# Three units' transposes of r and k moved from TensorE to DMA, the order of all steps changed, and the last output matmul cut into two column runs

## The chip, the cores and the metric

The kernel runs on one core of one Trainium2 chip. The metric is the device time of one execution in microseconds. A run of a kernel gives one such time; the times below are of several runs. A profile of one execution gives the rest: busy times of the five engines (TensorE or PE with its weight loads PEld, VectorE or DVE, ScalarE or ACT, GpSimd or POOL, SyncE or SP), what each instruction waited for, and the DMAs.

## The reference

Two parts follow one another. The first is a linear attention with decay (RWKV-5): per batch b and head h a 48 x 48 state is carried through 768 time steps. The second is a feed-forward block with a squared ReLU on the 3072 x 384 result.

```python
batch, n_heads, seq, head_dim = (4, 8, 768, 48)
for t in range(S):
    cur = np.einsum('bhd,bhe->bhde', u[None] * kt, vt)
    y[:, :, t] = np.einsum('bhd,bhde->bhe', rt, state + cur)
    state = w[None, :, :, None] * state + np.einsum('bhd,bhe->bhde', kt, vt)
...
n_tokens, d_model, d_ff = (3072, 384, 2048)
h = np.maximum(x @ w_in, 0.0)
return (h * h @ w_out).astype(np.float32)
```

Here x is y with the heads side by side. All inputs and the output are float32; the kernel computes its matmuls in bf16.

## The kernel before

**Units.** The 768 steps are cut into six chunks of 128, and each of the 4 batches gives one unit per chunk: 24 units of 128 tokens x 384 features. Unit i is chunk i // 4 of batch i % 4. Chunk by chunk the recurrence becomes matmuls. For a unit the steps are:

- `ld` (L320): r, k and v are loaded by SP, 192 KB each, into one of seven buffers each.
- `rh`, `kh` (L339, L336): r and k are scaled by powers of the decay and cast to bf16, on VectorE or GpSimd, into one tile `rk` with the heads padded to 64.
- The transposes of `rk` into `rkT`: either `T` (L363), eight 128 x 128 transposes on TensorE into a PSUM bank, followed by `Tc` (L260), a ScalarE copy of 128 x 1024 to SBUF; or `XB` (L369), one DMA transpose issued by SP, SBUF to SBUF. Before, units 0 to 8 and 11 use T and Tc, the other 14 use XB.
- `A` (L376): eight matmuls k^T r per head, two PSUM banks; `Bm` (L384): masked copies on VectorE.
- `P0`, `P1`, `du`, `dv` (L342, L346, L349, L354): the term with u, elementwise, on VectorE and GpSimd. `vb` (L260, L262) casts v.
- `Y` (L392, L394): the unit's output from state and masked scores; `xs` (L411) adds dv. `U` (L403), `ts` (L421), `S` (L424) bring the state to the next chunk; `S0` (L418) does so for the first chunk.
- x has to be transposed too: `X` (L429) on TensorE with the copy `xTc` (L260), or `xX` (L436), a DMA transpose on SP.

**Feed-forward.** Units 0 and 1 are groups 0 and 1 by themselves, then two units make a group: 13 groups. `F1` (L445) computes 512 columns' worth of x @ w_in for a group into one of two banks, `re` (L453 on ScalarE, L455 on VectorE) takes the ReLU, `sq` (L460 on ScalarE; L464, L462 on VectorE) the square, and `F2` (L472) accumulates a quarter of h*h @ w_out, four matmuls of 384 columns, for one unit into one of two output banks `bO`. After the fourth quarter `os` (L260 or L262) copies the bank to one of four SBUF buffers and `out` (L489) stores it. For the last unit, 22, `os` and `out` are split in two halves of 192 columns.

**Weights.** `lW` (L324) loads seven of the eight pieces of w_in in float32 by SP, `cW` (L260, L262) casts them to bf16; `W` (L333) lets GpSimd's queue load the eighth and all of w_out, cast on the way.

**What sets the order.** Nothing is scheduled by the framework: `ORDER` is a list of all steps, written out, each with its engine and its buffer (`XB.9:S/1` is the DMA transpose of unit 9, issued by SP, into rkT buffer 1). A loop at the end of the kernel emits the steps in the order of the list, and every engine runs its own steps in that order; semaphores make a step wait for its inputs and for its buffer to be free. An engine that waits holds up everything behind it in its queue. SP's queue carries the loads, the transposes and the outs; its DMAs share eight completion semaphores in turn, so that the ninth waits for the first to land. `Z` (L481) steps are matmuls of the identity on itself, which give no result; they fill TensorE's time during the start.

Of the kernel before, what the change touches and what calls it, by code (L numbers as in the profile page):

```python
# [32 lines left out]
sq.2.5:D2/5 re.2.7:A/4 S0.3:D F1.0.1:P/0 F1.2.3:P/1 re.0.1:D/0 F2.1.0:P/0 S0.1:D re.2.3:A/3 F1.1.1:P/0 sq.1.2:D2/6
sq.0.1:D2/7 ld.k.7:S/6 F1.2.0:P/1 re.1.1:A/5 F2.0.1:P re.2.0:A/0 sq.1.1:D2/8 F1.2.2:P/0 sq.2.4:A0/9 sq.2.0:D1/10
F2.1.1:P kh.4:D/4 F1.2.6:P/1 ld.v.5:S/4 rh.4:D P0.4:D/4 F2.1.2:P ld.r.7:S/6 re.2.2:D/5 P1.4:G F2.0.2:P re.2.6:D/1
sq.2.2:A0/11 F2.1.3:P ld.v.4:S/5 kh.5:G/5 sq.2.1:A0/12 sq.2.6:D1/13 F2.0.3:P os.1:A/0 du.4:D/4 ld.k.6:S/0 T.4:P/0
sq.2.3:A0/14 rh.5:D F2.2.0:P/0 os.0:A/1 P0.5:D/0 Tc.4:A/4 ld.r.6:S/0 T.5:P/3 P1.5:D F2.2.1:P kh.7:D/6 Tc.5:A/5
ld.v.7:S/6 A.4:P/1/2 du.5:D/0 F2.3.0:P/1 Bm.4.0:D/3 ld.k.9:S/2 A.5:P/0/3 vb.4:A/4 dv.4:G Bm.4.1:D/2 F2.3.1:P vb.5:A/5
ld.r.9:S/2 Bm.5.1:D/4 dv.5:G sq.2.7:A0/15 Y.4:P/1 Bm.5.0:D/5 F2.3.2:P rh.7:G ld.k.8:S/1 xs.4:D/4 U.4:P/2 Y.5:P/3
F2.2.2:P P0.6:G/1 ld.v.6:S/0 xs.5:D/0 X.4:P/0 ts.4:D/0 X.5:P/1 T.7:P/3 xTc.4:A/1 kh.6:D/1 ld.k.15:S/3 F2.2.3:P xTc.5:A  # L40
rh.6:D vb.7:A/6 U.5:P/2 P1.6:D F1.3.0:P/0 Tc.7:A/6 ld.k.10:S/4 ts.5:D/1 F1.3.1:P/1 kh.9:D/2 re.3.0:A/0 ld.v.9:S/2
T.6:P/0 P0.7:D/2 os.2:A/2 A.7:P/1/2 S.5:D re.3.1:A/5 ld.r.8:S/1 F2.3.3:P du.6:D/2 P1.7:G Tc.6:A/0 Bm.7.1:D/0 F1.3.3:P/0
sq.3.0:A0/16 rh.9:G ld.r.10:S/3 os.3:D/3 F1.3.4:P/1 re.3.3:A/2 Bm.7.0:D/1 A.6:P/3/0 P0.9:G/3 du.7:D/1 re.3.4:A/1
XB.9:S/1 F1.3.5:P/0 Bm.6.1:D/3 sq.3.1:A0/17 dv.7:G F1.3.6:P/1 Bm.6.0:D/2 re.3.5:A/3 F2.5.0:P/0 dv.6:G vb.6:A/7
ld.k.12:S/5 sq.3.3:A0/18 Y.7:P/2 out.3:S kh.10:D/3 re.3.6:A/4 Y.6:P/1 ld.v.8:S/3 S.4:G xs.7:D/1 F1.3.2:P/0 sq.3.5:A0/19
xs.6:D/2 F1.3.7:P/1 ld.v.11:S/1 kh.8:D/0 re.3.2:A/0 kh.15:D/4 U.6:P/0 X.6:P/3 sq.3.2:A0/20 X.7:P/2 rh.8:D F2.4.0:P/1
ld.r.12:S/4 re.3.7:A/5 rh.10:D F2.5.1:P xTc.6:A/2 sq.3.4:D2/21 P1.9:D xTc.7:A U.7:P/1 T.8:P/3 vb.9:A/2 out.0:S P0.8:D/4
F1.4.0:P/0 ts.6:D/1 ld.k.11:S/0 Tc.8:A/2 P1.8:G ts.7:D/0 F1.4.4:P/1 ld.r.13:S/5 du.9:D/3 re.4.0:A/2 F2.5.2:P kh.12:G/5
re.4.4:A/3 F1.4.6:P/0 ld.r.11:S/0 sq.3.6:A0/23 sq.3.7:D2/22 vb.8:G/3 du.8:D/4 A.9:P/2/0 sq.4.4:A0/24 A.8:P/1/3 S.6:G
re.4.6:A/0 F2.5.3:P ld.v.10:S/5 Bm.8.1:D/4 F1.4.3:P/1 dv.8:G Bm.8.0:D/5 os.5:A/3 ld.k.13:S/6 F1.4.5:P/0 Bm.9.1:D/1  # L50
re.4.3:A/1 dv.9:G Y.8:P/3 Bm.9.0:D/0 re.4.5:A/5 XB.10:S/3 F2.4.1:P P0.12:G/0 xs.8:D/3 sq.4.0:A0/25 Y.9:P/1 vb.11:A/1
kh.11:G/1 F1.4.1:P/1 xs.9:D/4 ld.v.13:S/4 X.8:P/0 F1.4.2:P/0 re.4.1:D/4 xTc.8:A/0 ld.r.15:S/6 F2.4.2:P rh.11:D
sq.4.1:A0/26 P1.12:D X.9:P/2 vb.10:A/0 F1.4.7:P/1 P0.10:D/1 ld.k.20:S/2 xTc.9:A sq.4.5:D2/27 F2.7.0:P/0 P0.11:D/2
re.4.7:A/3 ld.v.12:S/6 U.8:P/3 P1.10:D sq.4.3:A0/28 F2.4.3:P kh.13:D/6 re.4.2:A/2 F1.5.2:P/1 du.10:D/0 out.1:S os.4:A/1
rh.13:G sq.4.2:A0/29 ts.8:D/1 A.10:P/1/0 ld.k.17:S/1 F2.6.0:P/1 re.5.2:A/4 P1.11:G ld.k.14:S/5 F1.5.7:P/0 rh.12:G
F1.5.1:P/1 du.11:D/1 ld.k.16:S/4 re.5.7:A/5 T.11:P/2 rh.15:D re.5.1:A/1 F1.5.0:P/0 dv.10:G Bm.10.1:D/3 Tc.11:A/4
# [12 lines left out]
ts.12:D/1 ld.k.21:S/3 sq.6.6:A0/13 F2.9.3:P P1.18:G xs.13:D/3 sq.6.5:A0/15 ld.v.16:S/1 F2.10.0:P/1 Bm.14.1:D/2 dv.14:G
X.13:P/0 du.15:D/0 F2.10.1:P ld.r.20:S/4 P0.16:G/4 re.6.7:D/2 xTc.13:A Y.14:P/1 vb.15:A/6 F1.7.5:P/0 kh.20:G/6 xs.14:D/4  # L70
ld.k.22:S/6 os.9:A/0 F1.7.6:P/1 S.12:D A.16:P/2/3 xX.14:S/0 re.7.6:A/1 P1.17:G A.17:P/0/1 F2.11.0:P/0 sq.6.7:A0/16
Bm.17.1:D/1 sq.6.4:A0/17 S.13:G F1.7.1:P/1 ld.v.20:S/6 Bm.16.1:D/0 re.7.5:A/4 F2.11.1:P ld.k.19:S/5 Bm.17.0:D/2 dv.15:G
Y.15:P/1 re.7.1:D/3 ld.r.19:S/6 F1.7.0:P/0 xs.15:D/0 rh.20:G F1.7.3:P/1 re.7.0:A/0 ld.r.23:S/5 P1.16:D U.15:P/3
sq.7.1:A0/20 F2.10.2:P du.16:D/1 re.7.3:A/2 U.14:P/0 xX.15:S F1.7.2:P/0 P0.20:D/1 vb.16:A/3 dv.16:G Bm.16.0:D/3
sq.7.3:A0/18 F1.7.4:P/1 out.5:S re.7.2:A/5 rh.18:D F2.11.2:P vb.18:A/1 out.8:S sq.7.6:D2/21 re.7.4:A/3 F2.10.3:P
sq.7.5:D2/19 ld.r.21:S/2 kh.19:D/5 vb.17:A/2 F1.7.7:P/0 ld.k.23:S/1 sq.7.4:A0/22 rh.19:D Y.16:P/1 kh.22:D/4 re.7.7:A/2
Y.17:P/2 XB.19:S/4 xs.16:D/2 sq.7.2:A0/23 F2.11.3:P kh.21:D/2 os.10:A/3 F1.8.2:P/1 du.17:D/2 sq.7.0:A0/26 XB.18:S/6
ts.14:D/1 F1.8.0:P/0 dv.17:G re.8.2:A/1 F2.12.0:P/1 os.11:A/2 re.8.0:D/4 vb.20:G/0 sq.8.2:A0/25 F1.8.3:P/1 xX.16:S/1
# [31 lines left out]
    ld=["{0}{1}"],  # L110
# [7 lines left out]
def kernel(  # L118
# [66 lines left out]
    def bank(var, kind="b"):  # L185
        return banks[first[kind] + slot[var]]
# [85 lines left out]
    class Do:  # L272
# [206 lines left out]
        def Z(e, n, b):  # L479
            for _ in range(n):  # L480
                e.matmul(banks[b][:, 0:128], identity, identity, start=True, stop=True, skip_group_check=True)  # L481
# [60 lines left out]
```

## Time and profile before

| | |
|---|---|
| device time, median of 3 runs | 176.17 us (174.75, 176.17, 177.58) |
| span of the profiled execution | 174.6 us |
| what lies around its span | not listed; the fastest run is 0.15 us above it, the median 1.57 |
| TensorE busy | 164.3 us (94%), 1813 matmuls |
| of these F1 / F2 / T / A | 74.4 / 73.6 / 6.2 / 8.5 us busy |
| VectorE, ScalarE, GpSimd busy | 140.6, 109.4, 69.4 us |
| XB: issue to landing | 3.3 to 5.0 us, median 4.2, 14 times |
| SP's DMA queue | 26.20 MB, its packets 72.6% of 16 engines' span |
| first F1 / last matmul ends | 21.6 us / 171.07 us |

Busy time of an engine is the union of its instructions, which overlap by some tens of nanoseconds, so that counts times mean durations give more than the busy time. The chain that ended last is followed back from the last instruction through what released each step; it tells whose time the span is made of. The profile's times are from the start of the span.

### The profile page before, as it was taken

To read this page: it belongs to the slowest core of one execution; us is meant where nothing else is said; L and a number is where in the kernel's file an instruction comes from. 1 tells how busy PE (TensorE), PEld (TensorE's weight loads), DVE (VectorE), ACT (ScalarE), POOL (GpSimd) and SP (SyncE) were. 2 spreads that over 40 slices of the span, in tenths; PEclk is the share of its full clock that TensorE was granted. 3 is DMA by queue.
4 is the path that set the end of the run, shared out by engine and by line. 5 is a ranking of instruction groups with operands and counts; after the bars stand their busy time and mean duration, and the time that the engine had idled before them with its cause. 6 is when DMAs were issued, how large, how long until landed. Compare 5 with 4: busy or idle time off the path is not lost.

```text
span 174.6 us, 4605 instructions
## 1 busy us (share of the span) xinstructions
PE 164.3 (94%) x1813; PEld 127.1 (73%) x1813; DVE 140.6 (80%) x279; ACT 109.4 (63%) x203; POOL 69.4 (40%) x85
## 2 busy tenths in 40 slices
PE   3978599999999999999999999999999999999991
PEld 3967488866778777877767787777778677787760
DVE  5779677799899989999989898899988667853620
ACT  3578479549499987786677669669478142164410
POOL 5253834044366594925373960700950302000000
PEclk9999999999999999999999999999999999999999
DMA  4989999989799999999998989989931422110041
GB/s 99 228 194 240 320 200 237 207 155 213 144 205 177 231 217 165 233 157 252 152 214 187 195 164 220 160 196 230 164 94 26 158 90 71 24 45 4 0 165 61
DMA packets 102421, 28.36 MB, mean 162 GB/s; under 512 B 94840, under 2 KB 102400, under 8 KB 102400
## 3 DMA queue, kind: packets, MB, share of 16 engines
q1 hardware_dynamic: 100504, 26.20, 72.6%
q0 software_dynamic: 1744, 1.77, 6.3%
q8 instruction: 14, 0.23, 0.5%
q10 hardware_dynamic: 152, 0.10, 0.2%
q14 instruction: 7, 0.06, 0.1%
HBM read 20.46 MB, written 4.72 MB: 144 GB/s over the span
## 4 chain that ended last, share of the span: by engine, by line
PE 84%; DMA 6%; SPq 4%; POOL 1%; issue 1%; ACT 0%; DVE 0%; POOLq 0%
PE bank L472 36%; PE bank L445 36%; DMA wsa<-in_moe_w_in_dram 6%; SPq L320 4%; PE bank L376 3%; PE bank L394 2%; PE bank L392 2%; PE bank L403 2%; PE bank L363 2%; PE bank L429 1%; POOL W L262 1%; SPq L324 0%; POOL urow L218 0%; ACT vb L260 0%; DVE os L262 0%
## 5 line engine op out<-in xcount | busy, mean ns | idle before, releaser
L445 PE MATMUL bank<-xT,W 128*128 128x256 bf16 (+1 forms) x624 | 74.4, 264 | 2.3 <-ACT W L260 2.1
L472 PE MATMUL bank<-W,hq 128*128 128x384 bf16 x384 | 73.6, 326 | 0.0
L453 ACT ACTIVATE hr<-bank 128x512 bf16<-128x512 f32 x71 | 42.0, 597 | 36.8 <-PE bank L445 34.2
L445 PEld LDWEIGHTS <-W 128*128 128x128 bf16 x624 | 55.4, 98 | 12.6 <-ACT W L260 2.2
L472 PEld LDWEIGHTS <-hq 128*128 128x128 bf16 x384 | 35.6, 98 | 17.8
L460 ACT ACTIVATE hq<-hr 128x512 bf16<-128x512 bf16 x57 | 34.7, 629 | 2.5 <-DVE hr L455 2.2
L384 DVE TENSOR_TENSOR Bm<-bank,maskJT 128x512 bf16<-128x512 f32 x48 | 31.4, 682 | 3.1 <-PE bank L376 3.0
L346 POOL TENSOR_TENSOR P<-P,ub 128x384 f32<-128x384 f32 x14 | 15.2, 1087 | 30.2 <-DVE P L342 27.4
L354 POOL TENSOR_TENSOR dv<-ldv,du 128x384 f32<-128x384 f32 x19 | 16.4, 874 | 25.0 <-DVE du L349 21.0
L455 DVE TENSOR_SCALAR hr<-bank 128x512 bf16<-128x512 f32 x25 | 17.1, 688 | 11.2 <-PE bank L445 7.5
L464 DVE TENSOR_TENSOR hq<-hr 128x512 bf16<-128x512 bf16 x35 | 15.0, 456 | 1.7 <-ACT hr L453 1.7
L411 DVE TENSOR_TENSOR xs<-bank,dv 128x384 bf16<-128x384 f32 x24 | 13.2, 553 | 3.2 <-PE bank L394 2.5
L481 PE MATMUL bank<-identity 128*128 128x128 bf16 x139 | 11.1, 244 | 2.7 <-POOL identity masks.py:199 2.7
L260 ACT COPY os<-bank 128x384 f32<-128x384 f32 (+1 forms) x18 | 8.4, 469 | 8.1 <-PE bank L472 8.1
L342 POOL TENSOR_TENSOR P<-ldr,ldk 128x384 f32<-128x384 f32 x11 | 11.3, 1025 | 4.8 <-DMA ldr<-in_r_dram 4.8
L349 DVE TENSOR_REDUCE du<-P 128x8 f32<-128x384 f32 x24 | 12.9, 542 | 0.0
L260 ACT COPY rkT<-bank 128x1024 bf16<-128x1024 bf16 x10 | 10.1, 1016 | 3.4 <-PE bank L363 3.3
L481 PEld LDWEIGHTS <-identity 128*128 128x128 bf16 x139 | 9.8, 112 | 2.9 <-POOL identity masks.py:199 2.7
L424 POOL TENSOR_TENSOR S0W<-ts,WLm 128x384 bf16<-128x384 f32 x7 | 7.4, 1061 | 10.0 <-PE bank L472 6.7
L394 PE MATMUL bank<-vb,Bm 128*128 128x48 bf16 x192 | 10.8, 183 | 0.5 <-ACT vb L260 0.5
L394 PEld LDWEIGHTS <-Bm 128*128 128x128 bf16 x192 | 9.5, 96 | 1.5 <-issue 0.8
L260 ACT COPY xT<-bank 128x384 bf16<-128x384 bf16 x14 | 6.5, 478 | 5.1 <-PE bank L429 5.1
(62 smaller groups left out, 167.1 us busy)
## 6 DMA issues: line engine op xcount, KB each, us to landing
ldr<-in_r_dram SPq DMA_DIRECT2D x24, 192.0 KB, 3.8
ldk<-in_k_dram SPq DMA_DIRECT2D x24, 192.0 KB, 3.9
ldv<-in_v_dram SPq DMA_DIRECT2D x24, 192.0 KB, 3.6
out_dram<-os SPq DMA_DIRECT2D x23, 192.0 KB, 2.1
wsa<-in_moe_w_in_dram SPq DMA_DIRECT2D x7, 384.0 KB, 5.9
W<-in_moe_w_out_dram POOLq DMA_DIRECT2D x4, 384.0 KB, 7.6
rkT<-rk SPq DMA_TRANSPOSE x14, 4.2
W<-in_moe_w_in_dram POOLq DMA_DIRECT2D x1, 192.0 KB, 8.8
```

What stands on the lines that cost most here:

```text
L260: e.copy(o, a)
L346: e.tensor_mul(t, t, ub)
L354: e.tensor_mul(dvb[slot[f"dv{i}"]], loaded("v", i), t)
L384: e.tensor_mul(Bmb[slot[f"Bm{i}{h}"]], heads(bank(f"bA{i}{h}"), 128), mask_b)
L394: e.matmul(y[:, hc, D * h : D * (h + 1)], m[h][:, hc, :], vb[:, 2 * hc + h, :], start=(c == 0), stop=True, skip_group_check=True,)
L445: e.matmul(hp[:, fi, :], W1[f // 2][:, c, 128 * (f % 2) : 128 * (f % 2 + 1)], xt[:, c, :], start=(c == 0), stop=(c == CCH - 1), skip_group ...
L453: e.activation(hr, hp, AF.Relu)
L455: e.tensor_scalar_max(hr, hp, 0.0)
L460: e.activation(hq, hr, AF.Square)
L464: e.tensor_mul(hq, hr, hr)
L472: e.matmul(bank(f"bO{i}", "bO")[:, 0:d_model], hqb[slot[f"hq{g},{f // m}"]][:, at : at + L], W2[q][:, f % 4, :], start=(f == 0), stop=(f = ...
L481: e.matmul(banks[b][:, 0:128], identity, identity, start=True, stop=True, skip_group_check=True)
```

## The change

Three things, all in one file.

1. Units 7, 8 and 11 lose `T` and `Tc` and get `XB`: 24 matmul transposes and 3 ScalarE copies out, 3 DMA transposes on SP in (17 in place of 14).
2. `ORDER` is a new list. Nearly every step has another place, and many another engine: `kh` 13 times on VectorE and 11 on GpSimd (19 and 5 before), `rh` 15 and 9 (18 and 6), `P0` 16 and 8 (13 and 11), `dv` 4 and 20 (5 and 19), `re` 21 times on VectorE and 75 on ScalarE (25 and 71), squares 28 on VectorE and 68 on ScalarE (39 and 57), `os` 11 on VectorE and 14 on ScalarE (7 and 18), `cW` 4 on ScalarE and 3 on GpSimd (6 and 1), `vb` 17 on ScalarE, 5 on GpSimd, 2 on VectorE (19, 3, 2). Ten of the outs go to GpSimd's queue (none before). The number of Z matmuls stays 139. During the start, `ld.v.1` comes earlier on SP's queue, `wc` (two small loads of the decay) earlier, `ld.v.3` later, behind `lW.0.7` and `lW.0.4`.
3. Unit 22's four F2 steps become two `F2c` steps: columns 256 to 383 over all 16 pieces of h, in one output bank, then columns 0 to 255 in the other. The halves of `os` and `out` follow these columns (256 and 128 wide; 192 each before).

The pools, buffers and all other functions stay as they are. The diff, with ORDER cut to its places named here:

```diff
-T.7:P/3 ... Tc.7:A/6 ... T.8:P/3 ... Tc.8:A/2 ... T.11:P/2 ... Tc.11:A/4
+XB.7:S/6 ... XB.8:S/1 ... XB.11:S/4
...
-lW.0.6:S/0 ld.v.1:S/0 ld.k.3:S/3 ld.v.3:S/1 lW.0.1:S/1 ld.r.3:S/3 ld.v.0:S/2 ld.v.2:S/3 lW.0.0:S/2 lW.0.5:S/3 lW.0.7:S/0 lW.0.4:S/1 wc:S
+wc:S lW.0.6:S/0 lW.0.0:S/2 ld.v.0:S/2 lW.0.1:S/1 lW.0.5:S/3 ld.v.2:S/3 lW.0.7:S/0 lW.0.4:S/1 ld.v.3:S/1 lW.0.3:S/2
...
-F2.22.0:P/0 ... F2.22.1:P ... F2.22.2:P F2.22.3:P os.22.0:A/2 os.22.1:D out.22.0:A out.22.1:S
+os.23:A/1 out.18:S out.23:S F2c.22.1:P/1 os.22.1:D/3 F2c.22.0:P/0 os.22.0:A out.22.1:S out.22.0:A
...
-    F1=["bH{0},{1}"], os=["os{0}"], Wk=["WkP"], Wt=["WtP"],
+    F1=["bH{0},{1}"], F2c=["bO{0}{1}"], os=["os{0}"], Wk=["WkP"], Wt=["WtP"],
...
+        def F2c(e, i, h):
+            g, j = group_of[i]
+            n = len(GROUP[g])
+            m = 4 // n
+            c = part(h)
+            for f in range(FCH):
+                at = L * n * (f % m) + L * j
+                e.matmul(
+                    bank(f"bO{i}{h}", "bO")[:, c],
+                    hqb[slot[f"hq{g},{f // m}"]][:, at : at + L],
+                    W2[f // 4][:, f % 4, c],
+                    start=(f == 0), stop=(f == FCH - 1), skip_group_check=True,
+                )
...
         def os(e, i, half=None):
             c = part(half)
-            copy(e, osb[slot[f"os{i}"]][:, c], bank(f"bO{i}", "bO")[:, c])
+            o = f"bO{i}" if half is None else f"bO{i}{half}"
+            copy(e, osb[slot[f"os{i}"]][:, c], bank(o, "bO")[:, c])
...
     def part(half):
-        return slice(0, d_model) if half is None else slice(d_model // 2 * half, d_model // 2 * (half + 1))
+        return slice(0, d_model) if half is None else (slice(0, 256), slice(256, d_model))[half]
```

The first six ORDER lines show steps of the two lists, with all steps between them left out.

## The prediction

> **What bounds the kernel now.** I read the page first (busy shares, then the chain that ended last), then the chain's shares by line, TensorE's waits, busy time by stretch, and last the timeline of the start and of the end.
>
> ```profile
> span 174.6 us, 4605 instructions
> PE 164.3 (94%) x1813; PEld 127.1 (73%) x1813; DVE 140.6 (80%) x279; ACT 109.4 (63%) x203; POOL 69.4 (40%) x85
> ```
> ```profile
> by line: PE bank L472 36.2%; PE bank L445 35.7%; DMA wsa<-in_moe_w_in_dram 6.3%; SPq L320 4.0%; PE bank L376 3.4%; PE bank L394 2.2%; PE bank L392 2.0%; PE bank L403 1.9%; PE bank L363 1.5%; PE bank L429 1.2%; issue 1.0%; POOL W L262 0.5%;
> ```
> ```profile
> PE bank L481 <- POOL identity masks.py:199: 2.7, 1, 2.7
> PE bank L445 <- ACT W L260: 2.1, 1, 2.1
> PE bank L363 <- DVE Bm L384: 0.6, 1, 0.6
> PE bank L394 <- ACT vb L260: 0.5, 2, 0.3
> PE bank L376 <- ACT rkT L260: 0.4, 2, 0.2
> PE bank L445 <- POOL W L262: 0.3, 1, 0.3
> ```
> ```profile
> 45.00:65.00 20.00, 20.00 (x249) 15.90 (x245) 18.99 (x36) 17.70 (x34) 12.19 (x15) 1.00 1.03 197
> 65.00:85.00 20.00, 20.00 (x226) 15.47 (x223) 19.15 (x36) 15.91 (x33) 10.28 (x11) 1.00 1.14 204
> 145.00:165.00 20.00, 20.00 (x167) 15.21 (x165) 12.76 (x27) 7.00 (x13) 0.02 (x1) 1.00 0.11 32
> ```
>
> The columns of the last fence are stretch, its length, then TensorE, its weight loads, VectorE, ScalarE and GpSimd busy, the granted clock, DMA share and GB/s. The chain is 84% TensorE, 146.7 us of 174.6. All its waits stand before 25 us, where weights arrive; from there it is busy in every stretch at clock 1.00. A busy PE is not PE at its peak, so I also added up the pieces: (624-96) x 109 ns plus 96 x 55 ns of F1, 384 x 163 ns of F2 and the small matmuls give 147 us from the first F1 at 21.6 to the last matmul at 171.07, which is 149.4 us. Some 2 us are gaps. So **TensorE's own work bounds the kernel from 25 us on; VectorE is nearly full beside it (19 of 20 us); the start is bound by arriving weights.**
>
> **The change, part by part.** All sums are on the profiled 174.6 us, which is 0.15 below the fastest run shown and 1.57 below their median of 176.17. I carry differences over to the median.
>
> *T removed (3 units).* The chain's share of L363 is 1.5%, 2.62 us for the six units transposed there after 25 us: 0.437 us per unit, or 8 x 54.6 ns. Three units: **-1.31 us** on the bound engine. Three Tc (L260, mean 1016 ns) leave ScalarE, -3.05 us, beside other work: nothing.
>
> *XB added (3), on SP.* The row of the 14 there are:
>
> ```profile
> L369 SPq DMA_TRANSPOSE rkT<-rk x14: 1237/1542/2622, 51.6 to 123.6; - x14
> DMA to landing us min/median/max: 3.3/4.2/5.0
> ```
>
> SP is busy issuing for 1.5 us each; queued behind are loads and later transposes. SP loses ten outs (about 0.55 us each) and gains three XB (+4.6 us), so its sum falls. What matters is whether a transpose lands before A (L376) reads it. I give each step a **place**: the TensorE time of all steps listed before it in ORDER (F1 0.66, F2 0.65, T 0.44, A 0.30, Y 0.335, U 0.17, X 0.18, Z 0.056 each, all from the chain's rows). In the kernel before, places foretell issue times: XB of units 9, 10, 15 and 17 have places 41.1, 53.1, 68.8, 81.4, and the trace has them at
>
> ```profile
> 51.59 1.64 SPq L369 DMA_TRANSPOSE rkT<-rk  x1
> 63.46 2.62 SPq L369 DMA_TRANSPOSE rkT<-rk  x1
> 79.09 1.70 SPq L369 DMA_TRANSPOSE rkT<-rk  x1
> 92.41 1.25 SPq L369 DMA_TRANSPOSE rkT<-rk  x1
> ```
>
> always 10.3 to 11.0 us later. From XB's place to A's place the kernel before has 5.4 to 14.7 us, all over the landing's 5.0. The new order has 4.7, 3.3, 2.3, 2.3, 4.1 for units 7 to 11, 3.6 for 13, 2.9 for 14, 1.6 for 17, 3.6 for 19 and 3.9 for 21. Taken literally the shortfalls against 4.2 us are 1.9 (8 and 9 together, whose A are neighbours), 1.9, 0.1, 0.6, 1.3, 2.6, 0.6, 0.3: **9.3 us** of waiting. But the new list is not sorted by time (P0.17 stands at 94.9 though its inputs are there at about 90; out.16 at 155 though os.16 is at 130), and following inputs and SP's queue, most can go earlier: XB.17 waits behind xX.12, which needs xs.12 (place about 81.2), so it goes at 83 and lands at 87, where A.17 stands at 87.1; XB.9 goes at about 44.5 and lands at 48.7 against 50.3; XB.11 needs kh.11 at 57.1 and lands at 61.3 against 61.9. Left are several arrivals within half a microsecond of their use. Bounds 0 and +9.3; nearest to the first by this tracing: **+0.5**.
>
> The Trainium skill (VectorE: DVE Perf Modes, sections "The three transpose paths" and "Rules for kernel authors") speaks against the change: a 128x128 transpose belongs on TensorE if PSUM may be its destination, at 390 ns against 1309 ns by DMA. By its figures one XB of eight blocks would be an estimated 10.5 us, and the three added ones would come 5.8, 7.2 and 6.4 us late by their places, +19.4 us in the sum. The trace disagrees with that size: all eight land in 4.2 us.
>
> *Engine loads.* By counts and row means VectorE loses 9.5 us (kh -6 x 633 ns, rh -3 x 575, squares -11 x 430, their busy time over their count; re -4 x 688, dv -1 x 558; P0 +3 x 606, os +4 x 553). ScalarE gains 1.6 (Tc and copies off; squares +11 x 609, re +4 x 597). GpSimd gains about 17.5 (kh, rh, casts; ten outs). Over the whole span each stays under TensorE. By stage, though, VectorE's steps with places 30 to 50 sum to 23.5 us, against 22.5 before, and its busy total is 0.92 of such a sum since neighbours overlap: 21.7 us in 20. It must lag some 1.7 there, against 0.7 before, and steps off by the same amount in 60 to 80. Bounds 0 and +1.7 less what the lists already lead: **+0.2**.
>
> *Ten outs on GpSimd.* Nearest rows: its weight DMAs take 771 ns to issue and 7.6 us to land (384 KB, DMA share over 1); the same out from SP lands in 2.1 us. Behind an out wait kh, rh, dv of its queue, at 0.8 us each; and an os slot comes free only when its out has landed. os.11 (place 97.8) reuses the slot of out.8 (issued at about 91), os.12 (108.3) that of out.4 (about 104). At 2.1 us both are free in time; at 7.6 os.12 comes 3.7 us late. I take 2.1, the same transfer: **0**; the other end is a rival.
>
> *The start.* Of it the timeline shows
>
> ```profile
> 21.63 1.51 PE L445 MATMUL bank<-xT,W 128*128 128x128 bf16 x24 [2.06 <-ACT W L260]
> 24.15 0.51 PE L445 MATMUL bank<-xT,W 128*128 128x128 bf16 x6 [0.27 <-POOL W L262]
> ```
>
> Loads landed at 4.7 us (0.39 MB), 9.2 (1.18), 15.0 (2.56), 17.4 (3.15) and 23.2 (4.33), read off what waited for them. With the new order on that curve W_in pieces 0 and 1 are there at 15.0 and 17.4, F1.1.0 follows X.0 at about 20.0 (-1.6), and piece 7 is cast at 23.1 (-1.0). But ld.v.3 now stands behind lW.0.7 and lW.0.4 (4.72 MB, some 25 us), and Y.3 needs it on TensorE's queue: at 25.7, where its place of 15.0 would like 24.3. The shift (time less place) is then 10.7 us against 10.5 before: the gain is given back. GpSimd's own weight DMAs go 1.2 to 2 us later than before, behind vb.2 and cW.0.3, and with their 7.6 us to land are there 1 us or less before use. Bounds -1.2 (v3 by 24) and +1.5 (by 26.5, or W.1.3 late): **0**.
>
> *The end.* Before:
>
> ```profile
> 171.09 0.32 ACT L260 COPY os<-bank 128x192 f32<-128x192 f32 x1 [4.72 <-PE bank L472]
> 171.44 0.35 ACTq L489 DMA_DIRECT2D out_dram<-os  x1
> 171.44 0.36 DVE L262 COPY os<-bank 128x192 f32<-128x192 f32 x1 [2.39 <-ACT os L260]
> ```
>
> VectorE's half waits for ScalarE's (one PSUM bank), and its out goes last, 0.76 us after the last matmul. F2c puts the halves in two banks: 16 matmuls of 128 columns (56 ns each, as the F1 of one unit: 0.90 us), then 16 of 256 (1.72); together +0.02 to F2's 2.60. Columns 256 to 383 are copied under the second run; then one copy of 256 columns (between 319 ns for 192 and 477 for 384: 0.37) and its out: 0.42 us after the last matmul. **-0.3**.
>
> Sum: -1.31 + 0.5 + 0.2 + 0 + 0 + 0.02 - 0.3 = **-0.9 us**: 173.7 on the profile, **175.3** on the median.
>
> **Rivals.** (1) *Transposes land after their A*: TensorE, in order, waits at L376 with all of F1 and F2 behind it. It decides wherever the way from XB's issue to A is under 4.2 us. For it: the leads above, a DMA share already at 1.0 to 1.14, 3.3 to 5.0 us spread. Against: no transpose was late before. Half the literal shortfall, 4.7 in place of 0.5, gives 179.5; all of it 184. (2) *GpSimd's outs land late* (7.6 us): os.12 holds VectorE for 3.7 us, behind it rh.21, XB.21 and A.21: about 178.5. Against: half the size and no cast. (3) *The start's gain is kept* and 0.5 of the old gaps close: -1.31 - 0.3 - 1.2 - 0.5 = -3.3, 172.9. For it: F1 does start earlier. (4) *The change doesn't do what it says*: TensorE's freed 1.31 us become gaps, because VectorE (9.25 to 9.67 of every 10 us from 45 to 95) sets the pace: 175.9 with the end's gain. Against: it loses 9.5 us.
>
> **How the numbers follow.** Forecast 0.50 (173.9 to 177.0), late transposes 0.17, late outs 0.08, start kept 0.14, gain absorbed 0.11. The range runs from the kept start, 172.7, to just above half the late transposes, 180.0; left out are the literal 9.3 us and a start better than its bound. A measurement of this kernel can tell about 2%, 172.65 to 179.69. Faster needs more than rival 3's middle: 0.10. Slower: most of rival 1 and a part of 2: 0.18. Same: 0.72.
>
> **What would show it.** Right: L363 has 56 matmuls; TensorE's waits at L376 on a DMA under 1 us; first F1 near 20 us, a wait for ldv or vb near 25; no ScalarE wait before VectorE's last copy. Wrong: waits at L376 of over 1 us behind rkT's DMA, or at os behind out_dram, or gaps at Bm and xs. The sum is most easily upset by DMA arrivals, which I placed by one curve of one run.

## The result, and the profile after

The changed kernel takes 185.09 us (median of 4 runs, 184.64 to 185.99) against 175.95 for the kernel before beside it (4 runs, 174.75 to 177.58): a ratio of 1.056, 95% interval 1.051 to 1.060. It is slower by 9 us, and the forecast (175.3, range 172.7 to 180.0) missed on the far side. All ratios, and the medians and ranges of the experiments below, leave out disturbed runs (over 1.5% above the fastest of their kernel), and a ratio can differ a little from the quotient of two medians.

The page of the changed kernel, span, busy shares, TensorE's clock in 40 slices and DMA issues with their time to landing:

```profile
span 182.9 us, 4597 instructions
PEclk9999999999999998799999999999999999999999
out_dram<-os SPq DMA_DIRECT2D x13, 192.0 KB, 2.9
out_dram<-os POOLq DMA_DIRECT2D x10, 192.0 KB, 3.4
rkT<-rk SPq DMA_TRANSPOSE x17, 3.7
```

The chain's shares by line, and TensorE's waits (us in total, times, longest):

```profile
by line: PE bank L445 28.1%; PE bank L472 23.1%; DMA out_dram<-os 6.1%; ACT hr L453 4.9%; DMA ldv<-in_v_dram 3.7%; SPq L320 3.5%; DVE Bm L384 3.4%; issue 3.1%; PE bank L376 2.3%; DMA ldk<-in_k_dram 2.0%; PE bank L394 1.7%; PE bank L403 1.6%
```
```profile
PE bank L445 <- ACT hr L453: 1.9, 5, 0.6
PE bank L472 <- ACT os L260: 1.9, 1, 1.9
PE bank L403 <- DVE xs L411: 1.3, 1, 1.3
PE bank L394 <- POOL vb L262: 0.9, 1, 0.9
PE bank L376 <- ACT rkT L260: 0.8, 1, 0.8
PE bank L445 <- DVE hr L455: 0.7, 1, 0.7
PE bank L403 <- DVE Bm L384: 0.6, 1, 0.6
```

And the same three stretches as before (length, TensorE, weight loads, VectorE, ScalarE, GpSimd busy, clock, DMA share, GB/s):

```profile
45.00:65.00 20.00, 19.77 (x234) 15.42 (x231) 19.19 (x36) 14.69 (x29) 11.32 (x12) 1.00 1.01 199
65.00:85.00 20.00, 17.57 (x183) 12.81 (x182) 13.16 (x26) 14.34 (x29) 10.19 (x11) 0.91 0.85 163
145.00:165.00 20.00, 20.00 (x173) 14.82 (x171) 11.76 (x23) 9.44 (x17) 3.95 (x6) 1.00 0.18 55
```

The chain was 84% TensorE; now F1, F2 and the small matmuls make 62% of it, and an out's landing, the ReLU and loads stand in it. No wait of TensorE ends at a DMA transpose. The waits at L445, L472 and L403 are on banks and buffers: F1 for the ReLU that empties its bank, F2 for `os`, U for the reader of its bank. VectorE has 13 us of work in the 20 between 65 and 85: it is kept waiting, not full.

To see where the time went I took the shift (start less place) of every TensorE step from the trace and added up its growth from the first F1 to the last matmul:

| growth of the shift at | before | after |
|---|---|---|
| F1 that takes over a bank filled less than 0.72 us of TensorE work ahead | 0 | 4.69 (11 steps) |
| other F1, waiting for `re` | 0.10 | 1.12 (6) |
| U in a bank that Bm or xs still reads (U.2, U.13, U.14) | 0 | 2.49 (3) |
| F2.7.0, waiting for os.5, which waited for out.3 to land | 0 | 2.03 (1) |
| four steps from 73 to 76 us, at half clock | 0 | 1.69 (4) |
| F2.23.3, waiting for the last square, and F2c behind it | - | 0.53 (1) |
| all else, net | 1.80 | 0.91 |
| sum | 1.90 | 13.46 |

That is 11.56 more. Against it stand the first F1, 1.70 earlier in shift, 1.32 less work on TensorE, and 0.2 at the end: 8.3, the difference of the spans (182.9 - 174.6).

**The largest single wait**, in the timelines of GpSimd, ScalarE and TensorE of the changed kernel:

```profile
64.77 0.83 POOL L354 TENSOR_TENSOR dv<-ldv,du 128x384 f32<-128x384 f32 x1
65.55 0.62 POOL L504 DMA_DIRECT2D out_dram<-os  x1
```
```profile
70.18 0.48 ACT L260 COPY os<-bank 128x384 f32<-128x384 f32 x1 [2.76 <-DMA out_dram<-os]
```
```profile
70.71 1.03 PE L472 MATMUL bank<-W,hq 128*128 128x384 bf16 x4 [1.88 <-ACT os L260]
```

out.3 is issued at 65.55 and lands at 70.16; os.5 shares its buffer and holds ScalarE for 2.76 us; F2.7.0 needs the bank that os.5 empties. In ORDER out.3 and os.5 stand at the same place, with no TensorE step between (place 55.2); in the kernel before 8.7 us lie between them. Then the clock of TensorE halves:

```profile
71.00:72.00 1.00, 0.95 (x11) 0.63 (x10) 0.00 (x0) 0.97 (x3) 1.00 (x2) 1.00 1.23 246
72.00:73.00 1.00, 1.00 (x8) 0.52 (x5) 0.00 (x0) 1.00 (x3) 0.21 (x1) 0.59 1.01 179
73.00:74.00 1.00, 1.00 (x11) 0.62 (x11) 0.27 (x1) 0.90 (x3) 0.00 (x0) 0.50 0.87 158
74.00:75.00 1.00, 1.00 (x7) 0.73 (x5) 1.00 (x3) 0.30 (x1) 0.00 (x0) 0.50 1.27 278
75.00:76.00 1.00, 1.00 (x10) 0.78 (x9) 1.00 (x3) 0.82 (x2) 0.00 (x0) 0.71 1.11 290
```

The seventh number after the lengths is the clock: half from 72.2 to 75.6.

**A small wait that comes often** is that of an F1 for its bank, here F1.5.3 (TensorE's timeline, then ScalarE's re.5.5):

```profile
78.39 0.82 PE L445 MATMUL bank<-xT,W 128*128 128x256 bf16 x6
79.14 0.40 PE L376 MATMUL bank<-rkT 48*128 48x128 bf16 x8
79.95 0.81 PE L445 MATMUL bank<-xT,W 128*128 128x256 bf16 x6 [0.41 <-ACT hr L453]
```
```profile
79.30 0.60 ACT L453 ACTIVATE hr<-bank 128x512 bf16<-128x512 f32 x1 [0.96 <-PE bank L445]
```

F1.5.5 and F1.5.3 both use bank 1, and only A.11 (0.3 us) stands between them; ScalarE starts at once, but a ReLU takes 0.60. ScalarE had been idle: it is not a lack of an engine.

### The profile page after: what moved, and what is told of

It is laid out like the page before. It is cut to its first block, busy times and chain, and to the rows that moved or that the text cites. A ratio compares the mean times of both kernels' runs of the same rounds, so it can differ in the third digit from the quotient of the medians.

```text
span 182.9 us, 4597 instructions
## 1 busy us (share of the span) xinstructions
PE 166.8 (91%) x1805; PEld 128.4 (70%) x1805; DVE 135.7 (74%) x261; ACT 112.0 (61%) x207; POOL 85.7 (47%) x106
## 4 chain that ended last, share of the span: by engine, by line
PE 62%; DMA 12%; DVE 8%; ACT 7%; SPq 4%; issue 3%; POOL 1%; ACTq 0%; DVEq 0%; POOLq 0%
PE bank L445 28%; PE bank L472 23%; DMA out_dram<-os 6%; ACT hr L453 5%; DMA ldv<-in_v_dram 4%; SPq L320 3%; DVE Bm L384 3%; PE bank L376 2%; DMA ldk<-in_k_dram 2%; PE bank L394 2%; PE bank L403 2%; PE bank L392 1%; PE bank L486 1%; ACT hq L460 1%; DVE hr L455 1%
## 5 line engine op out<-in xcount | busy, mean ns | idle before, releaser
L445 PE MATMUL bank<-xT,W 128*128 128x256 bf16 (+1 forms) x624 | 76.0, 267 | 3.3 <-ACT hr L453 1.9
L472 PE MATMUL bank<-W,hq 128*128 128x384 bf16 x368 | 70.8, 326 | 2.3 <-ACT os L260 1.9
L445 PEld LDWEIGHTS <-W 128*128 128x128 bf16 x624 | 56.5, 99 | 16.4 <-issue 5.7
L453 ACT ACTIVATE hr<-bank 128x512 bf16<-128x512 f32 x75 | 44.3, 596 | 26.1 <-PE bank L445 24.8
L472 PEld LDWEIGHTS <-hq 128*128 128x128 bf16 x368 | 34.3, 98 | 19.8 <-issue 2.1
L460 ACT ACTIVATE hq<-hr 128x512 bf16<-128x512 bf16 x68 | 40.3, 624 | 5.6 <-DVE hr L455 5.4
L354 POOL TENSOR_TENSOR dv<-ldv,du 128x384 f32<-128x384 f32 x20 | 18.2, 910 | 15.4 <-DVE du L349 9.9
L455 DVE TENSOR_SCALAR hr<-bank 128x512 bf16<-128x512 f32 x21 | 14.3, 687 | 13.5 <-PE bank L445 9.0
L260 ACT COPY os<-bank 128x384 f32<-128x384 f32 (+1 forms) x14 | 6.6, 469 | 14.1 <-PE bank L472 8.0
L339 POOL TENSOR_TENSOR rk<-ldr,Wt 128x384 bf16<-128x384 f32 x9 | 9.6, 1069 | 9.0 <-DMA ldr<-in_r_dram 9.0
L336 POOL TENSOR_TENSOR rk<-ldk,Wkhat 128x384 bf16<-128x384 f32 x11 | 11.4, 1038 | 4.2 <-DMA ldk<-in_k_dram 3.9
L464 DVE TENSOR_TENSOR hq<-hr 128x512 bf16<-128x512 bf16 x24 | 12.3, 537 | 0.1
L342 POOL TENSOR_TENSOR P<-ldr,ldk 128x384 f32<-128x384 f32 x8 | 8.3, 1047 | 7.5 <-DMA ldr<-in_r_dram 3.8
```

The lines of the kernel that those rows point to most:

```text
L260: e.copy(o, a)
L354: e.tensor_mul(dvb[slot[f"dv{i}"]], loaded("v", i), t)
L445: e.matmul(hp[:, fi, :], W1[f // 2][:, c, 128 * (f % 2) : 128 * (f % 2 + 1)], xt[:, c, :], start=(c == 0), stop=(c == CCH - 1), skip_group ...
L453: e.activation(hr, hp, AF.Relu)
L455: e.tensor_scalar_max(hr, hp, 0.0)
L460: e.activation(hq, hr, AF.Square)
```

## The experiments

My theory after the two traces: the loss lies in the new order, not in the three DMA transposes. The rivals are named with each run. The kernel before ran beside each call, at 175.2 to 175.7 us.

**1 and 2. The change's small parts alone, in the old order.**

```diff
-T.7:P/3 ... Tc.7:A/6 ... T.8:P/3 ... Tc.8:A/2 ... T.11:P/2 ... Tc.11:A/4
+XB.7:S/6 ... XB.8:S/2 ... XB.11:S/4
```

Each XB stands right behind its rh. The second run has the F2c end as well, as in the change's diff.

> The kernel before, with one part of the change alone: T and Tc of units 7, 8 and 11 leave the order, and XB of the same units stands on SP right behind their rh; nothing else moves. Theory 1 (the loss is in the new order, not in the three DMA transposes): 24 TensorE transposes less, 1.3 us, against up to 0.5 us of waiting at A.8, whose rh ends only 4.4 us ahead of it: 174.5 to 175.5 against a kernel before at 175.9, a ratio of 0.990 to 0.998. Rival A (the three transposes themselves cost what was lost, through SP's queue, whose loads they hold up by about 1.5 us each, or by landing late): 180 or more, with A.7, A.8 or A.11 waiting for DMA or a VectorE stage waiting for loads.

> The kernel before with two parts of the change: the three DMA transposes as in the run ahead, and the last F2 in two column runs with its copies and outs as in the changed kernel. Theory 1: 0.3 us below the run with the transposes alone, so 174.2 to 175.2, a ratio of 0.987 to 0.996, and the span ends 3.2 to 3.4 us after the last matmul instead of 3.5. Rival A: 180 or more, as there. If the two runs are level within 0.2 us, the tail is worth nothing.

Measured: 177.58 us, ratio 1.011 (1.007 to 1.015), for the transposes alone; 177.09 us (6 runs, 175.69 to 178.32), ratio 1.004 (0.998 to 1.010), with the end. Neither theory had this: the transposes do not bring what the change lost, but they cost 1.9 us where I had expected a gain. TensorE's waits and its timeline in the first run:

```profile
PE bank L374 <- DMA rkT<-rk: 1.3, 2, 0.9
```
```profile
82.82 0.40 PE L374 MATMUL bank<-rkT 48*128 48x128 bf16 x8 [0.86 <-DMA rkT<-rk]
```

(L374 is A.) The shift grows by 0.61 at A.8, 0.95 at A.12 and 0.50 at A.18: XB.8 lands at 60.87, just behind its A; XB.12 and XB.18 were there before and now land too late, because SP comes to them later (XB.12 issued at 79.08 in place of 75.31). So SP's queue had no room for three more transposes, whose issuing took 1.6 to 1.9 us each. The worth of the F2c end can't be told from these two runs: their intervals overlap.

**3. The new order with the transposes back on TensorE.**

```diff
-XB.7:S/6 ... XB.8:S/1 ... XB.11:S/4
+T.7:P/2 ... Tc.7:A/6 ... T.8:P/2 ... Tc.8:A/1 ... T.11:P/2 ... Tc.11:A/4
```

> The changed kernel with the transposes of units 7, 8 and 11 back on TensorE (T on a free PSUM bank and Tc on ScalarE, a few steps ahead of A) and the three XB gone from SP; the rest of the new order stays. Theory 1: the loss stays and the 1.3 us of TensorE come back on top; SP without three transposes frees 1.4 us each and ld.v.9 can land earlier, which may take 1 us off the wait at F2.7.0: 184.5 to 187, a ratio of 1.048 to 1.062. Rival A (the DMA transposes are the cause): 175 to 178, a ratio of 0.995 to 1.012.

Measured: 185.3 us, ratio 1.052 (1.043 to 1.062). The loss stays without the three transposes: rival A falls for the changed kernel. In the new order they are worth nothing that these intervals can tell: TensorE's time for T comes back, and the wait at F2.7.0 shrinks from 2.0 to 0.3 us.

**4. out.3 alone, earlier on GpSimd.**

```diff
-Y.9:P/1 out.3:G S.7:D xs.8:D/3 re.4.1:A/4 XB.10:S/3 os.5:A/3
+dv.6:G out.3:G ... Y.9:P/1 S.7:D xs.8:D/3 re.4.1:A/4 XB.10:S/3 os.5:A/3
```

> The changed kernel with one step in another place: out.3, still issued by GpSimd, stands right behind dv.6 instead of behind P0.12's stage, where GpSimd has nothing else to do after 54.1 us, so that it should land near 57 us instead of 70.2. Theory 1: os.5 no longer waits for it, the wait of 2.0 us at F2.7.0 goes, and with it the stretch of half clock after it and the 1.7 us lost there: 181.3 to 183.2, a ratio of 1.030 to 1.041. Rival B (the order has no slack anywhere, so that a wait removed is met by the next one): at least 184.3, with the same shift of the steps behind unit 10. If only the wait goes and not what follows it, 183 to 183.3.

Measured: 181.55 us, ratio 1.028 (1.019 to 1.037): 3.5 us gained by the place of one DMA. It is issued at 55.5 and lands at 60.0. TensorE is busy without a gap where it stood idle, at full clock (the last line is another stretch, of the start):

```profile
68.00:70.00 2.00, 2.00 (x37) 1.85 (x36) 0.88 (x2) 2.00 (x5) 1.18 (x1) 1.00 1.24 236
70.00:72.00 2.00, 2.00 (x21) 1.45 (x18) 1.92 (x5) 1.75 (x5) 0.00 (x0) 1.00 0.84 158
72.00:74.00 2.00, 2.00 (x26) 1.54 (x24) 1.80 (x5) 1.96 (x5) 1.88 (x2) 1.00 1.08 185
19.50:22.90 3.40, 3.40 (x35) 3.20 (x35) 0.69 (x1) 1.86 (x5) 2.85 (x5) 0.50 0.79 211
```

So this trace has its half clock too, but at the first F1: by F2.4.3, the step ahead of F2.7.0, its shift is 14.5 us against 12.6 in the changed kernel. From there to F1.5.3 the shift grows by 1.4 us, against 4.9: 3.5 less, of which the wait itself is 2.0 and the rest stands in the steps that had run at half clock.

**5. F1's banks in turn.** Only the number of the bank changes, at 26 F1:

```diff
-F1.5.5:P/1 ... F1.5.3:P/1 ... F1.5.4:P/0
+F1.5.5:P/1 ... F1.5.3:P/0 ... F1.5.4:P/1
```

> The changed kernel with the PSUM banks of F1 given out in turn (0, 1, 0, 1 in TensorE's order, up to group 10); 27 of the F1 steps get the other bank and no step moves. In the kernel before no F1 stands less than 0.72 us of TensorE work behind the end of the F1 whose bank it takes over; in the changed kernel eleven do (0.17 to 0.65 us), and a re alone takes 0.6 to 0.7 us. Theory 2 (the loss is the sum of three things in the order: banks of F1 taken over too soon, 4.7 us in those eleven waits; out.3 too late for os.5, 3.5 us; U in banks that are still being read, 2.5 us): these eleven waits go, 185.1 - 4.7 = 180.4, between 179.5 and 182, a ratio of 1.020 to 1.035. Rival C (ScalarE is late with re whatever the bank, since squares, copies of v and os stand ahead of it): the waits move to the other bank's re, at least 184, a ratio of 1.046 or more.

**6. The same with out.3 early and three U later.**

```diff
-U.2:P/0 Bm.3.1:D/0 Z.4.4:P F1.1.3:P/0 ... F1.0.3:P/1 ld.k.4:S/4 X.2:P/2
+Bm.3.1:D/0 Z.4.4:P F1.1.3:P/0 ... F1.0.3:P/1 ld.k.4:S/4 X.2:P/2 U.2:P/0
...
-U.13:P/0 Bm.14.0:D/3 F1.6.5:P/1 ... U.14:P/0 P0.20:D/1 F1.7.3:P/1
+Bm.14.0:D/3 F1.6.5:P/0 U.13:P/0 ... P0.20:D/1 F1.7.3:P/0 U.14:P/0
```

> The changed kernel with three edits: F1's banks in turn as in the run ahead; out.3 right behind dv.6 on GpSimd; U.2 behind X.2, U.13 behind F1.6.5 and U.14 behind F1.7.3, so that each finds its bank read. The three DMA transposes, the ten outs on GpSimd and the rest of the new order stay. Theory 2: 185.1 - 4.7 - 3.5 - 2.5 = 174.4, between 173.5 and 177, a ratio of 0.986 to 1.006: level with the kernel before or a little faster. Rival C (engines behind TensorE are late anyway and take back what is opened): 178.5 or more, with waits for re, Bm or xs in other places.

In both runs two of the 96 ReLUs (re.8.4 and re.9.4) stand behind the F1 that takes over their bank and so read that step's columns: these two kernels do all the work, but their result is wrong (run 9 puts both ReLUs ahead). Measured: 182.75 us, ratio 1.041 (1.032 to 1.050), and 179.75 us, ratio 1.023 (1.015 to 1.031). The waits that I took away are gone from the traces, but only half of their sum came off the time: 2.3 of 4.7, and 5.3 of 10.7. In run 5, F2.7.0 simply waited longer for out.3 (2.53 us in place of 2.03), and F1.9.1 for xX.17 (1.24). In run 6 the largest waits that stayed behind the start end at DMAs:

```profile
PE bank L443 <- DMA xT<-xs: 1.2, 1, 1.2
PE bank L374 <- DMA rkT<-rk: 1.0, 1, 1.0
```

So theory 2 is right about what the waits are, and rival C about half of their price: the new order has other steps right behind those that I removed.

**7. The ten outs back on SP, each in its place.**

```diff
-out.3:G ... out.1:G ... out.7:G
+out.3:S ... out.1:S ... out.7:S
```

> The changed kernel with the ten outs that GpSimd issues given back to SP, each in its place in the order. Theory 2 (out.3 came late through GpSimd's queue, where it stood behind dv.9, which waited for a load): SP reaches out.3 between ld.k.11 and XB.10, near 64.5 us, and it lands near 67.5, 2.7 us earlier than in the changed kernel, so the wait at F2.7.0 falls from 2.0 us to about 0 and what follows it goes too; against it SP issues ten more DMAs at 0.4 to 0.8 us each ahead of its loads and transposes, which can cost up to 0.95 us at an A each time, as the run of the transposes alone showed. 181.5 to 184.5, a ratio of 1.031 to 1.048. Rival D (outs on GpSimd are late wherever they stand, and cost in several places): 180 or less. Rival E (who issues them is of no matter): 184.7 to 186.

Measured: 184.51 us, ratio 1.049 (1.041 to 1.057), between theory 2 (up to 184.5) and rival E (from 184.7); the interval tells neither from the other. out.3 is issued by SP at 66.69 and lands at 71.04, 4.35 us later; from GpSimd it took 4.6. This trace, as that of run 4, has its half clock at the start (19.5 to 22.9), so TensorE is 2.0 us later here; against its steps the out comes about 1 us earlier, and F2.7.0 waits 0.9 us in place of 2.0. Who issues the outs matters little in the total; the place of out.3 brought 3.5 us. The Trainium skill (Trainium Kernel Development and Optimization, section "Key Constraints") says that the queues of SP, ScalarE and GpSimd share the same 16 DMA engines and that several issuers save issue time only; the trace agrees, with 4.35 against 4.6 us to land.

**8. The old order with less of the change:** XB for units 7 and 11, the F2c end, and five outs on GpSimd in their places.

```diff
-T.7:P/3 ... Tc.7:A/6 ... T.11:P/2 ... Tc.11:A/4
+XB.7:S/6 ... XB.11:S/4
...
-out.3:S ... out.0:S ... out.1:S ... out.2:S ... out.6:S
+out.3:G ... out.0:G ... out.1:G ... out.2:G ... out.6:G
```

> The kernel before with the DMA transposes of units 7 and 11 alone (unit 8, whose rh ends too near to its A, stays on TensorE), five outs (0, 1, 2, 3 and 6) issued by GpSimd in their places to make room on SP, and the last F2 in two column runs; no other step moves. The run of the three transposes alone lost 0.6 us at A.8, 0.95 at A.12 and 0.5 at A.18, the last two since SP came later to the transposes of units 12 and 18. Theory 2: with SP's room bought back those waits are 0 to 0.3 us, and 16 TensorE transposes (0.9 us) and 0.3 us of the end are gained: 174.5 to 175.6, a ratio of 0.990 to 0.998. If the room is not what was short: 176.5 or more, as the run with three transposes.

Measured: 175.61 us, ratio 0.999 (0.995 to 1.004): level, without the gain that theory 2 had foretold. With room on SP, XB.12 and XB.18 are in time again (80.72 for A.12 at 81.54, 113.13 for A.18 at 113.73), and unit 8, on TensorE, no longer waits: 2.0 us better than run 1. XB.7 is 0.5 us late.

**9. Run 6 with four more moves**, at the DMAs whose waits had come up.

```diff
-out.0:S ... ld.k.11:S/0 ... XB.10:S/3
+out.0:S ld.k.11:S/0 XB.10:S/3
...
-ld.k.21:S/3 ... ld.v.22:S/0 ... xX.16:S/1 ... xX.17:S
+xX.16:S/1 ... xX.17:S ld.k.21:S/3 ld.v.22:S/0
...
-lW.0.7:S/0 ... lW.0.4:S/1 ld.v.3:S/1
+ld.v.3:S/1 lW.0.7:S/0 ... lW.0.4:S/1
...
-F1.8.1:P/0 ... re.8.4:D/5
+re.8.4:D/5 F1.8.1:P/0
```

> The run with three edits (banks of F1 in turn, out.3 early, U.2, U.13 and U.14 later) with four more: re.8.4 and re.9.4 stand ahead of the F1 that takes over their bank; XB.10 and ahead of it ld.k.11 stand right behind out.0 on SP; xX.16 and xX.17 stand ahead of ld.k.21 and ld.v.22; ld.v.3 stands ahead of lW.0.7. In the trace of that run three DMAs on SP ended waits of TensorE that no edit had touched: XB.10 (1.14 us, at A.10), xX.17 (1.41, at F1.9.1) and ld.v.3 (1.2, at Y.3, of which 0.7 is shift against the kernel before). Theory 2 with this addition (the new order leaves the DMAs of SP no slack either, which its other waits covered): 179.75 - 1.1 - 1.4 - 0.7 = 176.5, between 175 and 178, a ratio of 0.997 to 1.013. Rival C (each wait taken away opens another): 178.8 or more.

Measured: 178.13 us (2 runs, 177.77 and 178.49), against 178.93 to 180.28 for the four of run 6: 1.6 us less where the edits were to bring 3.2, between theory 2 (up to 178) and rival C (from 178.8). Two runs don't settle more. The waits at A.10 and F1.9.1 are gone; U.8 now waits 1.28 us for Bm.10.1 in its bank, U.18 1.00 us for v of unit 18, whose load has kept its place on SP, and F1.1.2 1.1 us for a weight that ld.v.3 had pushed back. So rival C is right about these three.

**10. The reverse: close banks in the old order.** No step moves; F1's two banks change places from each of eight F1 on, which gives 25 F1 the other bank and puts eight close behind the F1 whose bank they take over.

```diff
-F1.10.0:P/0 ... F1.10.5:P/1
+F1.10.0:P/1 ... F1.10.5:P/1
```

> The kernel before with nothing moved; F1's two banks change places at eight F1 (F1.3.5, 4.6, 5.0, 6.6, 8.3, 8.4, 9.4 and 10.5), so that each of these takes over the bank of the F1 only 0.30 to 0.65 us of TensorE work ahead of it, as eleven do in the changed kernel. Theory 2: each then waits for that one's re, whose end in the trace of before lies 0.20 to 0.53 us behind the start of the F1, 2.65 us for the eight; TensorE has no slack to take it back: 175.6 + 2.65 = 178.2, between 177.5 and 179, a ratio of 1.011 to 1.020. Rival C (waits of that size are taken back further on, and the banks are only where lateness shows): within 0.8 us of the kernel before, a ratio below 1.005.

Measured: 179.19 us (177.61 to 179.27), ratio 1.019 (1.011 to 1.027), as a ratio where theory 2 had it and 0.2 us above its range. The trace has the eight waits where they were foretold, 0.19 to 0.57 us each, 2.70 in sum against 2.65:

```profile
134.69 0.81 PE L443 MATMUL bank<-xT,W 128*128 128x256 bf16 x6 [0.38 <-ACT hr L451]
```

This is the clean proof of that mechanism: no step moved, no engine got more work, and TensorE took nothing back. From the first F1 to the last matmul the shift grows by 2.6 us more than in the kernel before; the span of this trace is only 1.3 us longer because its first F1 starts 1.3 us earlier.

**11. The start of the new order.**

```diff
-U.2:P/0 ... X.2:P/2
+X.2:P/2 U.2:P/0
...
-lW.0.7:S/0 ... lW.0.4:S/1 ld.v.3:S/1
+ld.v.3:S/1 lW.0.7:S/0 ... lW.0.4:S/1
```

> The changed kernel with two edits in its first 25 us: U.2 stands behind X.2 as in the kernel before, so that TensorE has X.2 and two F1 between Y.2 and it and its bank is read by then, and ld.v.3 stands ahead of lW.0.7. Theory 2 (the start's gain of 1.6 us is lost again to U.2's bank, 1.45 us, and to v.3's late landing): 185.1 - 1.45 and up to 0.7 more, 182.9 to 183.9, a ratio of 1.040 to 1.050, with the first F1 still near 19.5 us. Rival (the wait at U.2 only stands in front of a later one for W or re, so that the next of them takes its place): 184.6 or more. If the weights lW.0.7 and later, which land later by ld.v.3's time, are what F1 of unit 0 and 1 wait for: 185 to 186.

Measured: 182.69 us (3 runs, 181.90 to 183.21), ratio 1.043 (1.032 to 1.053), as expected by the ratio and 0.2 us below the range in time. First F1 at 19.73; shift at F1.3 11.4 in place of 12.4. By F2.4.3 it is 11.5 in place of 12.6, which is 1.1 us of the 2.7 by which this trace is shorter than that of the changed kernel. The other 1.6 stand between F2.4.3 and F1.5.3: F2.7.0 waits 1.55 us in place of 2.04, and the clock stays at 1.00 behind it.

**12. What seemed worth keeping, in the old order.** Run 8 with T.7 and Tc.7 in place of XB.7, and lW.0.0 one DMA earlier.

```diff
-ld.v.2:S/3 ... lW.0.0:S/2
+lW.0.0:S/2 ld.v.2:S/3
```

> The kernel before with what the runs showed to be worth keeping: the DMA transpose of unit 11 alone (the one whose rh ends 7 us ahead of its A), five outs (0, 1, 2, 3 and 6) on GpSimd in their places to make room on SP, the last F2 in two column runs, and the weights lW.0.0, whose landing ends the wait of the first F1, one DMA earlier on SP (ahead of ld.v.2). No other step moves. Theory 2 (a gain on TensorE's path stays gained where the order around it keeps its slack): 0.44 us of transposes, 0.3 of the end, and 0.7 to 1.3 at the start: 175.7 - 1.4 to 2.0, so 173.7 to 174.5, a ratio of 0.988 to 0.994. Rival C (other waits take it back): 175.2 or more, a ratio of 0.997 or more. If the start's gain is lost again at Y.2, whose v lands later, 174.9.

Measured: 176.30 us (9 runs, 175.25 to 177.19), ratio 1.004 (1.001 to 1.007): no gain, rival C. The first F1 does start at 19.78, 1.85 us earlier, but the timelines of VectorE and TensorE show why that is lost:

```profile
18.37 0.69 DVE L382 TENSOR_TENSOR Bm<-bank,maskJT 128x512 bf16<-128x512 f32 x1
21.13 0.55 DVE L347 TENSOR_REDUCE du<-P 128x8 f32<-128x384 f32 x1 [2.07 <-POOL P L344]
21.60 0.68 DVE L382 TENSOR_TENSOR Bm<-bank,maskJT 128x512 bf16<-128x512 f32 x1
22.20 0.68 DVE L453 TENSOR_SCALAR hr<-bank 128x512 bf16<-128x512 f32 x1
```
```profile
22.34 0.35 PE L392 MATMUL bank<-vb,Bm 128*128 128x48 bf16 x7 [0.82 <-DVE Bm L382]
22.93 0.49 PE L443 MATMUL bank<-xT,W 128*128 128x128 bf16 x6 [0.24 <-DVE hr L453]
24.57 0.51 PE L443 MATMUL bank<-xT,W 128*128 128x128 bf16 x6 [1.15 <-POOL W L260]
```

v of unit 2 now lands at 19.58 (17.32 before); GpSimd's cast of it waits and holds P1.3, that holds du.3, and a Bm and re.1.0 stand behind du.3 on VectorE: Y.3 waits 0.82 us for the Bm and the second F1 of unit 1 another 0.24 for re.1.0. The same F1 then waits 1.15 us for a weight whose cast stands on GpSimd behind all this. So none of the kernels run is faster than the one before.

## Why the prediction was wrong

The forecast put three terms at or near nothing, and the loss stands in these three: the outs (0; a wait of 2.0 us, 3.5 when it was taken away), the engine loads (+0.2; 4.69 us of waits for banks of F1 and 1.04 for banks of U) and the start (0; +1.7, of which 1.57 are F1 banks counted in the 4.69).

**T removed, -1.31: right.** L363 has 56 matmuls, and the place sum is 1.32 us less.

**XB added, +0.5 with bounds 0 and 9.3: the low end was right.** TensorE's waits at L376 show no DMA transpose; rival 1 did not happen. The leads traced by hand were good, and the literal reading of places was not. Part of it was luck: XB.10 lands 3.2 us ahead of A.10 because TensorE is late by then; in run 6, where it is earlier, A.10 waits 1.0 us for it. Run 1 adds what the term did not hold: in the old order, where SP still issues all outs, the same three cost 3.2 us gross. Whether SP has room depends on the ten outs being elsewhere, a coupling that I had costed as two separate terms.

**Ten outs on GpSimd, 0: the wrong pairs.** I checked os.11 and os.12, because their outs go to GpSimd with kh, rh and dv behind them, and asked how long an out takes to land. The step that failed is the list of pairs. The shortest ways from an out to the `os` that takes its buffer over are 3.3 us of place in the kernel before; in the new order out.3 to os.5, out.13 to os.15 and out.16 to os.23 have none, and out.15 to os.17 has 0.3. Two of these four outs are SP's. At a landing of 2.1 to 4.6 us three of these four `os` wait for their out, 0.75 to 2.76 us, and os.23 finds its buffer free since its own F2 is late. The table carries 2.0 us for the first; moving that step alone brought 3.5. A pair with more room fails too: out.21 stands 3.3 us ahead of os.20 and takes 4.0 us to land, os.20 waits on VectorE, and behind it waits the square that the last F2.23 needs. That is the table's 0.53:

```profile
175.28 0.56 DVE L262 COPY os<-bank 128x384 f32<-128x384 f32 x1 [0.89 <-DMA out_dram<-os]
176.50 0.50 PE L472 MATMUL bank<-W,hq 128*128 128x384 bf16 x2 [0.36 <-DVE hq L462]
```

**The start, 0: the loads were right, a bank was left out.** First F1 at 19.53 (forecast 20.0), ld.v.3 at 24.0 (forecast 25). But U.2, moved to stand behind Y.2 in the same PSUM bank, waits for xs.2: 1.45 us. Two F1 of units 0 and 1 follow each other by 0.17 and 0.18 us in one bank: 1.57 more. Shift at F1.3: 12.4 against 10.7 before, so +1.7, a little beyond my upper bound of 1.5. Run 11's two edits took 1.1 us of it back in the trace; the rest of that run's gain of 2.4 us stands at F2.7.0 and in the clock behind it.

**Engine loads, +0.2 with bounds 0 and 1.7: the wrong question.** I summed busy time by stage. VectorE has less to do in the new order (4.9 us by its busy time, where 9.5 was forecast; ScalarE's +1.6 comes to 1.4 by the rows it is made of, and nothing hangs on either), and the kernel lost time all the same, because what counted was the way from one step to the one that needs its bank. A bank of F1 comes free one F1, one ReLU (0.60 us on ScalarE, 0.69 on VectorE) and some 0.1 us later; with under 0.72 us of other TensorE work between two F1 of one bank, TensorE waits. The kernel before has no such pair, the new order eleven: 4.69 us, and 1.04 more for U.13 and U.14 in banks still read. No term and no rival of the prediction held this, though ORDER shows it without any trace: step, bank and the TensorE work between them. Run 10 puts the price at 0.19 to 0.57 us each.

**The end, -0.3: right** within what the profile shows. The last copy is ScalarE's alone, and the span ends 3.3 us after the last matmul (3.5 before). Its worth in time is below what the runs can tell.

**The sum.** The forecast of -0.9 held two gains that came true and a string of terms near 0. Rivals 2 and 4 came nearest (an `os` held by an out; freed TensorE time becomes gaps), at the wrong step and for the wrong engine, and with prices of 178.5 and 175.9. The deeper error is the use of the shift. I took it as constant after the start, since it grows by only 1.9 us in the kernel before. That is the property of an order in which steps have slack: after 50 us, 2 of its 217 TensorE steps start within 0.2 us of their last input; in the new order it is 23 of 216. Runs 5, 6 and 9 show the other side: where no step has slack, a wait taken away was worth about half of what the traces had for it.

What stays open: what the new order could still give. After its seven edits (run 9) it stands at about 178 us, by two runs, and the remaining 2 to 3 us were not traced to one cause. Nor is it settled what the half clock costs: one of the four runs of the changed kernel had a mean clock of 1.00 and took 185.41 us like the others (0.991), and there is no trace of that run.

## What to carry to other kernels

When an order of steps is replaced, count reuse distances before engine loads: for every buffer and bank, the bound engine's work between the step that fills it, the one that empties it and the next one that takes it over, against the measured time of the emptying step (here 0.7 us for a ReLU, 2 to 4.6 us for an out to land). A step that is far from full engines can still hold the bound one, and one DMA in the wrong place costs more than all the matmuls saved. A transfer that moves to another queue should be costed together with what makes room for it there.

## What the runs showed of the hardware

The clock of TensorE fell to half after little idle time: in the changed kernel TensorE was busy 2.1 of the 4 us from 68 to 72, with one idle stretch of 1.9, and ran at 0.50 for the following 3.4 us. The Trainium skill (TensorE: Matmul & The Clock Gate, section "What's actually happening") gives an idle window of about 3.4 us for this; the length of the slow stretch agrees, but here less than a whole idle window was enough. In run 6 waits of 1.0 and 1.2 us did not do it, nor did the 2.06 us before the first F1 of the kernel before:

```profile
19.50:21.70 2.20, 0.14 (x4) 0.08 (x3) 0.93 (x2) 0.99 (x2) 1.80 (x3) 1.00 1.04 318
```

In all fourteen traces the stretches between the first change of the clock and the last are whole multiples of 3.41 us (3.41, 13.65, 64.85 and 167.25 among them), which suggests that what counts is how busy TensorE is within one such window. It was busy for 1.06 to 1.86 of the 3.41 us ahead of the half clocks inside a kernel (the changed one, runs 4, 5 and 7). Windows that no half clock followed go down to 1.58, so the edge lies near half a window. The 2.06 us of the kernel before are split over two windows, whose edge is at 20.25.

The landing time of a 192 KB out goes with the traffic more than with the queue: 3.0 us for out.3 from SP at 54.9 in the kernel before, at a DMA share of 0.88; 4.35 from SP at 66.7 and 4.6 from GpSimd at 65.6 in the new order, at 1.14 and 1.08; and 1.9 us for out.18 of the kernel before, at 0.27. It isn't the whole cause: out.16 of the changed kernel took 4.05 us from SP at a share of 0.3. The landing of lW.0.0, which the first F1 waits for, moved between 18.8 (run 8) and 20.7 us (the kernel before) with the same list up to there, so that the start of a single profile is good to 2 us only.
